# Retention into Fourier mixing with an MLP: the third batch goes to Strassen groups and a written order

## The chip, the cores and the metric

The kernel runs on one core of a Trainium2 chip. Its engines work in parallel: TensorE (PE in the profile; its weight loads are PEld), VectorE (DVE), ScalarE (ACT), GpSimd (POOL), and SyncE (SP), which here only issues DMAs. The metric is device microseconds of one execution; the time before is the median of three runs.

## The reference

Inputs are q, k, v of shape (4 batches, 8 heads, 768 rows, 64) and two MLP weights, 512 x 2048 and 2048 x 512, all float32.

```python
gamma = 1.0 - 2.0 ** (-5.0 - np.arange(H))
for t in range(S):                      # retention, per batch and head
    state = gamma * state + outer(k[t], v[t])
    y[t] = q[t] @ state / sqrt(D)
x = y with the heads side by side       # (4, 768, 512)
mixed = real(fft(fft(x, axis=1), axis=2))
u = x + mixed
un = (u - mean(u)) / sqrt(var(u) + 1e-6)          # per row
out = u + maximum(un @ w_ch1, 0) @ w_ch2
```

## The kernel before

**Attention.** The recurrence is done in six chunks of 128 rows, for two heads (a pair) at a time, four pairs per batch. `load_unit` brings q, k and v of a pair by DMA. `cast_unit` (POOL) makes f16 copies, `t_unit` transposes q and k (by PE in batches 0 and 1, by DMA from SP in batches 2 and 3). `a_unit` (L659) multiplies k and q of two chunks at a time into a PSUM tile `wkA`, and DVE multiplies that by a decay mask in float32 (`maskp`) into the f16 tile `atm`. `kv_unit` (L676) makes the states `s`: five matmuls, one ACT copy, four DVE steps. `y_unit` (L702) adds state part (ten small matmuls) and score part (twelve, reading `atm`), and ACT writes x.

**Mixing.** `fold_s`, `fold_d` and `fold_e` (DVE) fold x by its symmetries. `s1_unit` (L843) is the DFT over the sequence: six matmuls of 193 columns, four times per batch; ACT casts each result into `g`, and a reversed copy goes into `gr` (here on DVE). `s2_unit` (L993) is the DFT over the features for one block of 128 rows: four matmuls of `g` (row blocks 0 to 2) or `gr` (3 to 5), two ACT copies (`qn`), two DVE operations into `u`, two POOL additions of x. `norm_unit` (L1046) takes row statistics on DVE and writes `un` (mean minus u, f16) on ACT. `unT_unit` (L1071) transposes `un` into `unT`, by DMA from batch 2 on.

**MLP, batches 0 to 2.** `h_unit` (L1087) makes one of 16 hidden blocks for 384 rows, four matmuls of 384 columns; Relu is split between ACT (`ACT_ROWS`) and DVE. `ch_unit` (L1124) is a quarter of the second product for one block of 128 rows: four matmuls of 512 columns, and in the last quarter a DVE operation that scales by 1/std, adds u and leaves a tile `ob` for the output DMA.

**MLP, batch 3.** It goes by three groups of 256 rows. `hp_unit` (L1169) makes hidden blocks n and n + 8 for the group: eight matmuls of 256 columns and a Relu of 512 elements. The second product is a Strassen scheme: the group is seen as 2 x 2 blocks (two row blocks i and j, two halves of the hidden units), the weights likewise (two halves of the output columns). Seven products (`p_unit`, L1205) of eight 256-column matmuls each stand in for the eight of the plain form. The sums of hidden blocks are made by DVE (`hidden_sums`, L1193: s1, s2, s4 and a difference that overwrites a quarter of the hidden tile), those of weights once by DVE (`wsum_unit`, L1156: eight subtractions). After each product DVE adds its PSUM half, scaled, to u or to an output tile. Products 1, 6 and 7 add up in one PSUM half, so that product 6 waits until DVE has read product 1, and product 7 until it has read product 6.

**Order.** Every piece of work is a unit with a due time in batches: the hidden and product units of batch b (the "majors") are spread evenly over b to b + 1, and the next batch's attention and mixing lie between them at times given by tables. `emit` (L1387) sorts all units by due time and traces them in that order. A scheduler then orders each engine's instructions by priority and readiness as it foresees them; what a unit's wrapper `held` (L150) marks can't be moved ahead of the instruction traced before it on its engine. Before, `held` is around the casts and around everything of batch 3. Waits between engines are semaphores; an engine executes its queue in order. [...]

## Time and profile before

| what | us |
|---|---|
| three runs | 240.98, 240.98, 241.79 (median 240.98) |
| profiled execution | 240.73 |
| its span, first to last instruction | 238.7 |
| busy: PE, DVE, ACT, POOL | 225.4, 187.4, 125.3, 81.4 |

The span runs from the first to the last instruction of the program; the execution's own time is 2.0 us longer. In a group row of the profile stand line, engine, operation, output <- inputs and shapes, the count, the busy time in all, the mean ns of one, and the idle time of the engine just before. In the chain of work that ended last, each piece has its start, its length and its name; rows are merged when neighbours are of one kind.

### The profile page before, as it was taken

To read this page: it belongs to the slowest core of one execution; us is meant where nothing else is said; L and a number is where in the kernel's file an instruction comes from. 1 tells how busy PE (TensorE), PEld (TensorE's weight loads), DVE (VectorE), ACT (ScalarE), POOL (GpSimd) and SP (SyncE) were. 2 spreads that over 40 slices of the span, in tenths; PEclk is the share of its full clock that TensorE was granted. 3 is DMA by queue.
4 is the path that set the end of the run, shared out by engine and by line. 5 is a ranking of instruction groups with operands and counts; after the bars stand their busy time and mean duration, and the time that the engine had idled before them with its cause. 6 is when DMAs were issued, how large, how long until landed. Compare 5 with 4: busy or idle time off the path is not lost.

```text
span 238.7 us, 5575 instructions
## 1 busy us (share of the span) xinstructions
PE 225.4 (94%) x2135; PEld 155.3 (65%) x2135; DVE 187.4 (79%) x460; ACT 125.3 (52%) x273; POOL 81.4 (34%) x148
## 2 busy tenths in 40 slices
PE   0788999999999999999999999999999999999993
PEld 0356779756775646765567446655666468888893
DVE  8789887958898889986886829977895885867473
ACT  5989759674865444840247415822257326072430
POOL 8378802665300097850000826940002410220000
PEclk9999999999999999999999999999999999999999
DMA  7999999999999489979999577696100261031202
GB/s 179 233 270 239 237 206 207 210 251 248 241 235 208 72 191 221 203 138 132 249 279 218 116 161 203 130 138 156 53 3 0 45 154 25 3 110 23 91 0 91
DMA packets 100954, 36.80 MB, mean 154 GB/s; under 512 B 91456, under 2 KB 97984, under 8 KB 100928
## 3 DMA queue, kind: packets, MB, share of 16 engines
q1 hardware_dynamic: 96704, 32.25, 64.2%
q0 software_dynamic: 4224, 4.19, 10.6%
q8 instruction: 17, 0.28, 0.5%
q14 instruction: 9, 0.07, 0.1%
HBM read 27.26 MB, written 6.29 MB: 141 GB/s over the span
## 4 chain that ended last, share of the span: by engine, by line
PE 82%; DVE 6%; DMA 5%; ACT 2%; issue 1%; POOL 1%; SPq 0%; DVEq 0%; ACTq 0%
PE psc L1131 23%; PE psh L1092 21%; PE psh L1179 9%; PE ps L1231 5%; PE psh L1109 3%; PE wkA L667 3%; DMA qTz<-q16z 3%; PE ps L850 3%; DMA k<-in_k_dram 2%; PE wkY L721 2%; PE pq L1012 2%; PE ps L830 1%; DVE atm L539 1%; PE wkY L717 1%; PE wkK L686 1%
## 5 line engine op out<-in xcount | busy, mean ns | idle before, releaser
L1131 PE MATMUL psc<-w,ht 128*128 128x512 f16 x288 | 67.7, 379 | 0.0
L1092 PE MATMUL psh<-unT,w 128*128 128x384 f16 x320 | 59.5, 326 | 0.0
L1040 POOL TENSOR_TENSOR u<-u,x 128x256 f32<-128x256 f32 x21 | 13.3, 635 | 117.1 <-DVE u L1019 104.8
L1131 PEld LDWEIGHTS <-ht 128*128 128x128 f16 x288 | 27.3, 98 | 26.5
L1092 PEld LDWEIGHTS <-w 128*128 128x128 f16 x320 | 29.9, 98 | 15.9 <-DMA unT<-un 0.4
L1096 ACT ACTIVATE ht<-psh 128x384 f16<-128x384 f32 x46 | 22.3, 489 | 23.7 <-PE psh L1092 23.2
L670 DVE TENSOR_TENSOR atm<-wkA,maskp 128x512 f16<-128x512 f32 x36 | 23.6, 680 | 1.7 <-PE wkA L667 1.7
L1184 ACT ACTIVATE ht<-psh 128x512 f16<-128x512 f32 (+1 forms) x24 | 13.7, 571 | 15.6 <-PE psh L1179 11.0
L1179 PE MATMUL psh<-unT,w 128*128 128x256 f16 x192 | 21.6, 273 | 0.0
L1098 DVE TENSOR_SCALAR ht<-psh 128x384 f16<-128x384 f32 x34 | 18.7, 549 | 2.7 <-PE psh L1092 2.5
L1056 ACT ACTIVATE un<-u,stats 128x512 f16<-128x512 f32 x21 | 14.8, 717 | 10.7 <-DVE stats L1052 7.6
L1179 PEld LDWEIGHTS <-w 128*128 128x128 f16 x192 | 18.7, 98 | 2.1
L1135 DVE SCALAR_TENSOR_TENSOR ob<-psc,stats,u 128x512 f32<-128x512 f32 x18 | 13.4, 743 | 8.5 <-PE psc L1131 8.3
L696 DVE SCALAR_TENSOR_TENSOR s<-s,gk,wkK 128x128 f16<-128x128 f16 x48 | 16.1, 336 | 2.4 <-ACT s L692 1.6
L729 ACT ACTIVATE x<-wkY,gexp 128x384 f16<-128x384 f32 x24 | 12.9, 580 | 9.0 <-PE wkY L721 8.9
L1051 DVE BATCH_NORM_STATS2 bst<-u 128x6 f32<-128x512 f32 x21 | 14.4, 686 | 4.0 <-POOL u L1042 3.8
L1231 PEld LDWEIGHTS <-ht 128*128 128x128 f16 x152 | 14.1, 98 | 2.3 <-issue 0.6
L441 POOL TENSOR_SCALAR kd<-k,gexp 128x384 f16<-128x384 f32 x24 | 13.8, 585 | 3.3 <-DMA k<-in_k_dram 3.3
L667 PE MATMUL wkA<-qTz,kT 128*128 128x256 f16 x72 | 13.2, 273 | 0.3 <-DMA qTz<-q16z 0.3
L1042 POOL TENSOR_TENSOR u<-u,x 128x256 f32<-128x256 f32 x21 | 13.3, 635 | 0.0
L1014 ACT COPY qn<-pq 128x128 f32<-128x128 f32 x18 | 4.9, 274 | 15.0 <-PE pq L1012 15.0
L1203 DVE TENSOR_TENSOR ht<-ht 128x512 f16<-128x512 f16 (+2 forms) x21 | 8.1, 385 | 5.9 <-ACT ht L1184 5.6
(194 smaller groups left out, 400.9 us busy)
## 6 DMA issues: line engine op xcount, KB each, us to landing
q<-in_q_dram SPq DMA_DIRECT2D x16, 384.0 KB, 6.0
k<-in_k_dram SPq DMA_DIRECT2D x16, 384.0 KB, 5.6
v<-in_v_dram SPq DMA_DIRECT2D x16, 384.0 KB, 5.7
out_dram<-ob SPq DMA_DIRECT2D x23, 256.0 KB, 2.4
w<-in_moe_w_ch_dram POOLq DMA_DIRECT2D x8, 512.0 KB, 10.9
unT<-un SPq DMA_TRANSPOSE x15, 2.5
kT<-kd SPq DMA_TRANSPOSE x10, 3.0
qTz<-q16z SPq DMA_TRANSPOSE x8, 3.8
```

Source lines behind the costliest of these rows:

```text
L441: kc = nc.gpsimd.tensor_scalar(out=kd[:, :, h2, :], in0=k32[:, h2], scalar1=gkd[:, h0 + h2:h0 + h2 + 1], scalar2=1.0, op0=ALU.mult, op1=AL ...
L667: mm = nc.tensor.matmul(wk[:, c2], st["kT"][:, c, :], st["qT"][:, :, c, :], start=True, stop=True)
L670: nc.vector.tensor_tensor(out=st["atm"][:, 2 * part:2 * part + 2], in0=wk, in1=maskp[:, PAIR_ORDER[i]].unsqueeze(1).to_broadcast([P, 2, 2, ...
L696: nc.vector.scalar_tensor_tensor(out=s16[:, c], in0=s16[:, c - 1], scalar=gk2[:, hp:hp + 1], in1=wk[:, c - c0], op0=ALU.mult, op1=ALU.add)
L1051: nc.vector.bn_stats(bst, u[:, kb, :])
L1056: nc.scalar.activation(un, u[:, kb, :], AF.Identity, bias=stats[:, kb, 0:1], scale=-1.0)
L1092: nc.tensor.matmul(psh, w116[:, cb, fb * P:(fb + 1) * P], unT[:, cb, rt * 384:(rt + 1) * 384], start=(cb == 0), stop=(cb == 3))
L1096: nc.scalar.activation(ht16[:, fb, :], psh, AF.Relu, bias=0.0, scale=-1.0)
L1098: nc.vector.tensor_scalar(out=ht16[:, fb, :], in0=psh, scalar1=-1.0, scalar2=0.0, op0=ALU.mult, op1=ALU.max)
L1131: nc.tensor.matmul(psc, ht16[:, fb, rb3 * P:(rb3 + 1) * P], w216[:, fb, :], start=(fb == 0), stop=(fb == NFB - 1))
L1179: nc.tensor.matmul(psh[:, t], w116[:, cb, fb * P:(fb + 1) * P], unT[:, cb, g * 256:(g + 1) * 256], start=(cb == 0), stop=(cb == 3))
L1231: nc.tensor.matmul(dst, lhsT, rhs[:, c0:c1], start=bool(new and n == 0), stop=(n == 7), skip_group_check=True)
```

## The change

Batch 2 (`SEVEN = 2`, and all later ones) is now done by row groups too.

- Groups 0 and 1 of batch 2 take the seven products, group 2 takes the plain form by `cg_unit` (32 matmuls of 512 columns). Batch 2 then has 49 majors: per group 8 `hp`, one `rstd`, and 7 products or 8 plain quarters. Weight sums are due at 1.555 to 1.80 instead of 2.89 to 2.98, and go to `wide` (four of the former eleven input buffers) and to the unused tables `cd16`, `sd16`; seven input buffers remain for batch 3.
- In the groups all Relus are ACT's, hidden sums come after block 5 (blocks 0 to 5, 768 elements) and 7, and the products' order is 1, 2, 4, 6, 5, 7, 3 instead of 1, 4, 5, 6, 2, 7, 3. In batch 1 ACT also takes every Relu whose block is no multiple of 4 (27 of 32 instead of 18).
- Everything due from 2.0 on is `held` on PE, ACT, POOL and DVE.
- Batch 3's scores are read from PSUM by ACT, six reads of 256 elements a pair with the scale, and DVE masks all 1536 at once in f16. The copies into `gr` of that batch are ACT's.
- Row blocks 3, 4, 5 of batch 2 are mixed at 1.83 to 2.04 (before: within batch 2, 2.048 to 2.341); blocks 0 and 1 of batch 3 at 2.84 to 2.95 (before 2.728 to 2.815), block 2 at 3.005 to 3.15.
- Times of batch 3's attention are given one by one. With hp(b, g, n) falling due at b + k/49, the written order in batch 2 is, in group 1: a(3,2,0) 2.347, hp 0, a(3,2,1), hp 1, a(3,2,2), hp 2, kv(3,3), hp 3, a(3,3,0), hp 4, y(3,2), a(3,3,1), hp 5 2.449, a(3,3,2) 2.460, hp 6, hp 7, rstd, y(3,3) 2.530, product 1 2.531; in group 2: hp 5 2.776, s1(0,0) 2.780, hp 6, s1(1,0), s1(0,1), hp 7 2.816, s1(1,1) 2.820, rstd, s2(block 0) 2.840, plain quarter 0, s2(block 1) 2.860, quarters 1 and 2, statistics of block 0, quarter 3, statistics of block 1 2.930, its transpose 2.950, quarters 4 to 7, s2(block 2) 3.005, hp 0 of batch 3 3.021.
- There are two output tiles instead of three.

The diff, cut to its core:

```diff
-ON_ACT = {'q': (0, 1, 0), 'kv': (1, 1, 1), 'g': (0, 1, 1), 'gr': (0, 0, 0)}
+ON_ACT = {'q': (0, 1, 0), 'kv': (1, 1, 1), 'g': (0, 1, 1), 'gr': (0, 0, 1)}
+END7 = 0.75
+C7 = (-0.035, 0.025, 0.12, 0.22)
+T7 = (-0.02, 0.04, 0.185, 0.315)
+KV7 = (0.03, 0.11, 0.31, 0.39)
+A7 = ((0.04, 0.10), (0.12, 0.17), (0.33, 0.38), (0.41, 0.46))
+Y7 = (0.18, 0.305, 0.44, 0.53)
+F7 = (0.57, 0.60, 0.65, 0.67, 0.68, 0.70, 0.72)
+DA7 = (0.02, 0.07)
-LD0, LD1 = (0.223, 0.312), (-0.370, 0.140)
+LD0, LD1, LD2 = (0.223, 0.312), (-0.2425, -0.115, 0.0125, 0.14), (-0.2425, -0.115, 0.0, 0.06)
-WS = (-0.12, -0.02)
-LAST_MIX = {3: (0.0, 0.07, 0.09, 0.20), 4: (0.25, 0.34, 0.36, 0.45), 5: (0.37, 0.445, 0.51, 0.56)}
-SUMS = ((3, 7), (2, 5, 7))
+WS = (-0.48, -0.20)
+MIX = {2: {3: (-0.17, -0.11, -0.10, -0.05), 4: (-0.13, -0.06, -0.05, 0.00),
+           5: (-0.08, -0.01, 0.00, 0.04)},
+       3: {0: (-0.16, -0.09, -0.08, -0.07), 1: (-0.14, -0.07, -0.06, -0.05),
+           2: (0.005, 0.075, 0.105, 0.15), 3: (0.03, 0.115, 0.17, 0.20),
+           4: (0.25, 0.34, 0.36, 0.45), 5: (0.37, 0.445, 0.51, 0.56)}}
+SEVEN = 2
+PLAIN = ((2, 2),)
...
-    inp = pool("inp", 11)
+    inp = pool("inp", 7)
-    obp = pool("obp", 3)
+    obp = pool("obp", 2)
+    mask16 = gk5[:, 1].rearrange("p e c -> p (e c)").bitcast(f16)[:, 0:P]
...
-    def held(unit):
+    def held(unit, engines=("",)):
...
+                if not any(g in str(ins[n].engine) for g in engines):
+                    continue
...
+    wide = const.tile([P, 4, 2, NCH, D], f32, tag="wide")
+    def in_tile(name, b):
+        n = loads[0] % 11
+        loads[0] += 1
+        if b < B - 1 and n >= 7:
+            return wide[:, n - 7]
+        return inp.tile([P, 2, NCH, D], f32, tag="in32", name=f"{name}32")
...
             a_of[b, i] = mm
+            if b >= SEVEN:
+                for h2 in range(2):
+                    nc.scalar.activation(st["atm"][:, 2 * part:2 * part + 2, h2, :], wk[:, :, h2],
+                                         AF.Copy, bias=0.0,
+                                         scale=float(gam[2 * PAIR_ORDER[i] + h2] ** (-P)))
+                if part == 2:
+                    atm = st["atm"].rearrange("p c h t -> p (c h) t")
+                    nc.vector.tensor_tensor(
+                        out=atm, in0=atm, in1=mask16.unsqueeze(1).to_broadcast([P, 2 * NCH, P]),
+                        op=ALU.mult)
+                return
...
-            if fb in ACT_ROWS[rt]:
+            if fb in ACT_ROWS[rt] or b + 1 == SEVEN and fb % 4:
...
+    def cg_unit(b, g, t, part):
...
+            for fb in range(4 * part, 4 * part + 4):
+                nc.tensor.matmul(psc_of[0], hg[:, fb % 8, fb // 8, t * P:(t + 1) * P],
+                                 w216[:, fb, :], start=(fb == 0), stop=(fb == NFB - 1))
...
+            for t0, t1 in ((0, 1), (1, 2)) if n == 7 else ((0, 2),):
+                nc.scalar.activation(hg[:, n, t0:t1], psh[:, t0:t1], AF.Relu, bias=0.0,
+                                     scale=-1.0)
+            if (b, g) in PLAIN:
+                return
+            if n == 5:
+                hidden_sums(0, 6, (1, 2, 4, 3))
+            elif n == 7:
+                hidden_sums(6, 8, (1, 2))
...
         for e in ev:
-            e[3]()
+            (e[3] if e[0] < SEVEN else held(e[3], ("PE", "Act", "Pool", "DVE")))()
...
-        if b == B - 1:
+        if b >= SEVEN:
             for g in range(3):
-                majors += [held(hp_unit(b, g, n)) for n in range(8)]
-                majors.append(held(rstd_unit(b, g, 2)))
-                majors += [held(p_unit(b, g, k)) for k in (1, 4, 5, 6, 2, 7, 3)]
+                majors += [hp_unit(b, g, n) for n in range(8)]
+                majors.append(rstd_unit(b, g, 2))
+                if (b, g) in PLAIN:
+                    majors += [cg_unit(b, g, t, part) for t in range(2) for part in range(4)]
+                else:
+                    majors += [p_unit(b, g, k) for k in (1, 2, 4, 6, 5, 7, 3)]
...
+                for make, times in ((cast_unit, C7), (t_unit, T7), (kv_unit, KV7), (y_unit, Y7)):
+                    streams += [([make(b + 1, i)], b + t, b + t) for i, t in enumerate(times)]
```

More of the change, by code (lines that the diff above doesn't have):

```diff
@@ L1251, in run @@
                 add(right, ps, ri, right)
-            elif k == 5 and tail:
-                flat_dc = seven["dc"].rearrange("p t m -> p (t m)")
-                add(u[:, j, 0:384], flat_dc[:, 0:384], rj, u[:, j, 0:384])
-                add(u[:, j, 384:DM], seven["e"], rj, u[:, j, 384:DM])
             elif k == 5:
-                add(pair(u[:, j]), seven["dc"], rj, pair(u[:, j]))
+                for dst, c0, c1 in outs:
+                    uj = u[:, j, 256 + c0:256 + c1]
+                    add(uj, dst, rj, uj)
             elif k == 7:
@@ L1456 @@
             streams.append((sums, end + da[0], end + da[1]))
-            streams += mix_units(b + 1, [0, 1, 2], *(end + t for t in da[2:]))
+            if b + 1 < B - 1:
+                streams += mix_units(b + 1, [0, 1, 2], *(end + t for t in da[2:]))
     emit(streams)
```

134 lines of the change are left out of this document (76 added, 58 removed).

## The prediction

> **What bounds the kernel now.** I read the page first (busy shares, the chain's shares by engine), then busy time by stage, then the chain in order of time.
>
> ```profile
> PE 225.4 (94%) x2135; PEld 155.3 (65%) x2135; DVE 187.4 (79%) x460; ACT 125.3 (52%) x273; POOL 81.4 (34%) x148
> ...
> PE 82%; DVE 6%; DMA 5%; ACT 2%; issue 1%; POOL 1%; SPq 0%; DVEq 0%; ACTq 0%
> ```
>
> PE is busy 94% of the span and holds 82% of the chain. The stages, cut where PE turns from batch 0's first hidden units to batches 1, 2 and 3 (columns: busy us of PE, PEld, DVE, ACT, POOL, then granted clock and DMA):
>
> ```profile
> 90.40:142.40 52.00, 51.72 (x411) 31.27 (x409) 39.90 (x96) 22.74 (x55) 18.83 (x32) 1.00 0.97 189
> 142.40:194.40 52.00, 52.00 (x420) 31.99 (x420) 44.41 (x102) 22.41 (x53) 15.95 (x27) 1.00 0.46 99
> 194.40:235.00 40.60, 40.07 (x384) 35.66 (x382) 26.97 (x68) 17.03 (x36) 3.69 (x6) 1.00 0.15 49
> ```
>
> Batch 2, the stage that the change rewrites, has no idle PE at all (52.00 of 52.00). So the change can win there only matmul work, and every wait that it adds to PE's queue is added to the end. The matmul rates, from unbroken runs in the chain:
>
> ```profile
> 132.08 10.36 PE psc L1131 x48
> ...
> 163.74 0.28 PE wkK L686 x5
> ...
> 164.88 0.29 PE wkY L717 x10
> 165.17 0.35 PE wkY L721 x12
> ...
> 171.64 5.94 PE psh L1092 x36
> 177.58 0.51 PE ps L850 x6
> 178.30 1.56 PE ps L850 x18
> ...
> 183.57 0.23 PE pq L1012 x4
> ...
> 209.41 6.11 PE psh L1179 x56
> 215.53 6.23 PE ps L1231 x56
> ```
>
> A 512-column matmul takes 10.36/48 = 0.216 us, a 384-column one 5.94/36 = 0.165, a 256-column one 6.11/56 = 0.109; the seven products of one row group take 6.23. PE's waits in the second half of the span are two (columns: total us, times, longest):
>
> ```profile
> PE ps L1231 <- DVE u L1235: 0.4, 1, 0.4
> PE wkA L667 <- DMA qTz<-q16z: 0.3, 1, 0.3
> ```
>
> The first is batch 3's, behind a Strassen add; the second is batch 1's, behind a DMA transpose.
>
> **The change part by part.** *Matmul work.* Batch 2's second product now takes 96 x 0.216 = 20.7 us; afterwards two groups of seven products (2 x 6.2 = 12.4) and one plain group (32 x 0.216 = 6.9) take 19.3. The hidden layer keeps its columns: 128 x 0.165 = 21.1 becomes 192 x 0.109 = 20.9, no difference that I count. **Saved: 1.4 us.** Row blocks that move between batches change no matmul.
>
> [...]
>
> *Waits.* Before, units before batch 3 could be reordered by the scheduler; now each engine executes everything due from 2.0 on in written order. I lay the written order beside these durations:
>
> ```profile
> L670 DVE TENSOR_TENSOR atm<-wkA,maskp 128x512 f16<-128x512 f32 x36 | 23.6, 680 | 1.7 <-PE wkA L667 1.7
> ...
> L1056 ACT ACTIVATE un<-u,stats 128x512 f16<-128x512 f32 x21 | 14.8, 717 | 10.7 <-DVE stats L1052 7.6 <-issue 2.2 <-POOL u L1042 0.6
> L1051 DVE BATCH_NORM_STATS2 bst<-u 128x6 f32<-128x512 f32 x21 | 14.4, 686 | 4.0 <-POOL u L1042 3.8
> ...
> L1135 DVE SCALAR_TENSOR_TENSOR ob<-psc,stats,u 128x512 f32<-128x512 f32 x18 | 13.4, 743 | 8.5 <-PE psc L1131 8.3
> ...
> L1042 POOL TENSOR_TENSOR u<-u,x 128x256 f32<-128x256 f32 x21 | 13.3, 635 | 0.0
> ...
> L729 ACT ACTIVATE x<-wkY,gexp 128x384 f16<-128x384 f32 x24 | 12.9, 580 | 9.0 <-PE wkY L721 8.9
> L1184 ACT ACTIVATE ht<-psh 128x512 f16<-128x512 f32 x21 | 12.5, 597 | 14.8 <-PE psh L1179 10.2 <-issue 4.6
> ...
> L1019 DVE SCALAR_TENSOR_TENSOR u<-pq,g,qn 128x256 f32<-128x256 f32 x18 | 8.5, 475 | 4.3 <-PE psh L1092 2.5 <-ACT qn L1015 1.6
> ...
> L773 DVE TENSOR_TENSOR eo<-xab 128x768 f16<-128x768 f16 x12 | 6.1, 552 | 0.1
> ...
> L1015 ACT COPY qn<-pq 128x127 f32<-128x127 f32 x18 | 5.2, 287 | 0.0
> ...
> L1052 DVE BATCH_NORM_AGGREGATE stats<-bst 128x2 f32<-128x6 f32 x21 | 3.5, 173 | 0.1
> ...
> L861 DVE COPY g16r<-g 128x384 f16<-128x384 f16 x12 | 3.1, 261 | 3.0 <-ACT g L857 2.9
> ...
> L1165 DVE TENSOR_TENSOR wsum<-w,wsum 128x1024 f16<-128x1024 f16 x4 | 2.8, 688 | 0.1
> ...
> L1235 DVE SCALAR_TENSOR_TENSOR ob<-ps,stats,u 128x256 f32<-128x256 f32 x5 | 2.4, 482 | 0.9 <-PE ps L1231 0.7
> ...
> L358 ACT COPY csn<-csp 128x384 f16<-128x384 f16 x1 | 0.6, 616 | 0.0
> ```
>
> Instructions of one engine overlap a little. ACT's timeline shows by how much:
>
> ```profile
> 178.13 2.37 ACT L857 CAST g<-ps 128x386 f16<-128x386 f32 x4
> ...
> 201.42 0.38 ACT L1184 ACTIVATE ht<-psh 128x256 f16<-128x256 f32 x1 [0.28 <-PE psh L1179]
> 201.70 0.29 ACT L1066 ACTIVATE stats<-stats,epsT 128x2 f32<-128x2 f32 x1
> ```
>
> So 386-column casts follow each other after 2.37/4 = 0.6 us at most (0.55 with the overlap), a 256-column read of PSUM frees ACT after 0.28 (201.42 to 201.70), and a 512-column Relu, 597 ns long, after 0.56 to 0.6.
>
> (a) *Scores.* Per pair, three DVE products (0.68) become six ACT reads of 256 columns (0.28 each: 1.7 us) and one f16 mask of 1536 elements. No row shows that size; 768 elements take 0.55 and 1024 0.69, so the slope is 0.14 us per 256 and I take 0.95; bounds 0.69 (the 1024 row) and 2.04 (the rate of the f32 row, if the repeated mask loses the f16 rate). DVE gains 4 x (2.04 - 0.95) = 4.4 us in batch 2, ACT takes 6.8 more. DVE had 44.4 of 52 us, ACT 22.4, so there is room on average; what matters is order.
>
> (b) *The last y of batch 3's attention.* In group 1 PE's written order is a(2,0), h0, a(2,1), h1, a(2,2), h2, kv, h3, a(3,0), h4, y2, a(3,1), h5, a(3,2), h6, h7, y3, product 1, where h is eight matmuls (0.87), a two (0.22), kv 0.28, y 0.64. Counted from the first a, h5 ends at 7.26 and y3's score half comes up at 9.5. ACT has, to its fifth Relu, six Relus at 0.56 to 0.6, ten score reads at 0.28 to 0.3, one copy and two x writes at 0.5; it ends Relu 5 at 8.1 (never late) to 8.5 (waits counted). DVE then does Strassen sums of blocks 0 to 5, written behind h5: four of 768 elements, 2.1 us, and only then pair 3's mask, 0.95, written behind a(3,2). The mask ends at 11.2 to 11.6, y3 was due at 9.5: **1.7 to 2.1 us, I take 1.7**; 1.4 if the mask costs 0.69, 3.0 if it costs 2.04. y3 stands in front of product 1, so all PE work waits; no cover.
>
> (c) *Sequence DFT into feature DFT.* In group 2: h5, s1, h6, s1, s1, h7, s1, then s2 with nothing between. s2's fourth matmul reads the last s1's copy. From h5's start, PE has 4.9 us of work to the end of the last s1 (4 x 0.51 + 3 x 0.87, and 0.2 for the small sums between the rows at 177.58 and 178.30), 5.0 with the s2 matmuls that needn't wait. ACT's queue behind h6, which ends at 2.5, is Relu 6 (0.6), g, gr, g, gr (1.1 + 2 x gr), Relu 7 (0.6), g (0.6). The gr copies are new on ACT (261 ns on DVE; an f16 copy of that size took 616 on ACT): I take 0.45, bounds 0.26 and 0.62. The last g ends at 2.5 + 3.8 = 6.3, and with 0.2 for the way from PE to ACT and back at 6.5 (6.1 to 6.8): **1.5 us, 1.1 to 1.8.** In the old order PE had eight hidden matmuls between, and gr was DVE's.
>
> (d) *First hidden unit of batch 3.* Rows 0 to 255 come from s2 of blocks 0 and 1, written only at 2.84 and 2.86. From the end of block 1's s2: two ACT copies 0.6, two DVE adds of the L1019 kind 0.9, two POOL adds 1.3, on DVE the out add of row block 4 that is written ahead (0.7) and the statistics (0.9), on ACT the normalised rows (0.7), and the transpose, issue to landing:
>
> ```profile
> out_dram<-ob SPq DMA_DIRECT2D x23, 256.0 KB, 2.4
> ...
> unT<-un SPq DMA_TRANSPOSE x15, 2.5
> ```
>
> That is 0.6 + 0.9 + 1.3 + 0.7 + 0.9 + 0.7 + 2.5 = 7.6 us. PE has seven plain quarters of 4 x 0.216 and one s2 of 0.23, 6.3. **1.3 us** (0.6 without the out add, 1.9 with ACT's backlog from (c)).
>
> (e) *Product 6 behind product 1's add.* In group 0, DVE does the sums (2.1), the last sums (0.6), the mask of pair 1 (0.95) and then product 1's add, while products 2 and 4 give 1.75 us of cover: 0.4 us (0 to 0.6). In batch 3 the order 1, 2, 4, 6, 5, 7 replaces 1, 4, 5, 6, 2, 7: the wait of 0.4 behind L1235 loses 0.2 (0 to 0.4), as fewer adds now stand ahead of product 6's on DVE.
>
> (f) *At nothing.* Batch 1's 9 Relus go to ACT, which has 52.0 - 22.7 = 29 us free there. Batch 2's blocks 3 to 5 (5.4 us of DVE) and the weight sums (8 x 0.69 = 5.5) move into batch 1's second half, which 4 Relus leave. DVE's 39.9 of 52 hides it; if it doesn't, block 1's transpose for batch 2 is late, 0 to 1.5 us. Batch 3's twelve loads now share seven buffers, so the last five wait for the casts of pairs 0 and 1; the loads began long before they are needed:
>
> ```profile
> 108.45 0.57 SPq L199 DMA_DIRECT2D q<-in_q_dram x1
> ```
>
> That is 34 us ahead of batch 2, and hides them; a late one delays a DMA transpose, which cost 0.3 in the one case above. The transposes of pairs 2 and 3 have 7 and 6 us of PE work between their issue and their readers. Two output tiles do where three were: one is written every 16 x 0.216 = 3.5 us at most, and its DMA lands after 2.4.
>
> **Sum:** -1.4 + 1.7 + 1.5 + 1.3 + 0.4 - 0.2 = +3.3 us on the profiled execution's 240.73 (span 238.7 and 2.0 around it): **244.0**. The median of the runs shown, 240.98, lies 0.25 above that execution. With all low ends (1.4, 1.1, 0.6, 0, -0.4) +1.3, 242.0; with all high ends (3.0, 1.8, 1.9, 0.6, 0, and 1.5 from (f)) +7.4, 248.1.
>
> **The rivals.** *Covered (faster).* PE's matmul work decides, because ACT and DVE run ahead of it: y3's mask lands before h7 ends and the s1 copies are out before h7's Relu. It decides if (b), (c) and (d) together stay under 1.4 us, which needs the mask ahead of the sums or ACT at half the time per read. For it: PE idles nowhere in batches 2 and 3 now. Against it: that was with free order. -1.4 - 0.2: **239.1**. *A wash.* (b) alone or (c) with (d) alone stands: 240.73 - 1.6 + 2.0 = **241.1**. *Crowded.* DVE saturates in batch 1 (1.5, from (f)) and the mask runs at the f32 rate (1.3 more in (b)): **246.8**. *Not what it says:* with 98 ns a weight load (PEld 35.7 of 40.6 in batch 3) 256-column matmuls could be load-bound; then nothing is saved and the forecast is 245.4; the 0.109 above already holds this, so it has no chance of its own.
>
> *Clock.* Where PE has no work, the granted clock falls, as the last slice shows:
>
> ```profile
> 235.00:240.00 5.00, 0.00 (x0) 0.00 (x0) 0.31 (x2) 0.00 (x0) 0.00 (x0) 0.89 0.24 80
> ```
>
> Two waits close together, (c) and (d), could do the same; 0.89 over the 5 us that follow costs 0.6, so **244.6**. [...]
>
> **How the numbers follow.** Forecast 0.58, covered 0.14, wash 0.18, crowded 0.07, clock 0.03. A measurement of this kernel can tell 0.5% (1.2 us) from no change: below 239.8 is faster, above 242.2 slower. Of the forecast, 0.02 falls below 242.2. So faster 0.14, same 0.20, slower 0.66. The range leaves out some of the covered case and the last of the crowded: 239.8 to 246.6.
>
> **What would show it.** Right: in batch 2 PE idles behind DVE atm for over 1.4 us once, behind ACT g for over 1 us before a pq matmul, and behind the unT transpose before the first hidden unit of batch 3; psc matmuls fall to 224. Wrong: PE busy over 51 us of that stage, or new waits elsewhere (transposes of q and k, input loads, output tiles).

## The result, and the profile after

The changed kernel takes 247.93 us (median of four runs, 247.32 to 250.01) against 240.98: a ratio of 1.0298, interval 1.0232 to 1.0364. That is slower, as forecast, but by 7 us instead of 3.3, and 1.3 above the end of the range. The profiled execution took 247.62 us, its span is 245.7 instead of 238.7.

First the busy times on the page of the changed kernel, and three of its groups (columns as before: count, busy us, mean ns, idle time ahead):

```profile
PE 226.8 (92%) x2247; PEld 166.9 (68%) x2247; DVE 178.7 (73%) x437; ACT 150.6 (61%) x351; POOL 87.3 (36%) x148
...
L700 ACT ACTIVATE atm<-wkA 128x256 f16<-128x256 f32 x48 | 16.2, 397 | 5.1 <-PE wkA L695 5.1
...
L705 DVE TENSOR_TENSOR atm<-atm,gk 128x1536 f16<-128x1536 f16 x8 | 8.2, 1022 | 9.6 <-ACT atm L700 9.6
...
L466 POOL TENSOR_SCALAR q16z<-q 128x384 f16<-128x384 f32 x14 | 10.0, 731 | 10.8 <-DMA q<-in_q_dram 10.5
```

DVE lost 8.7 us of work and ACT took 25.3 more. The counts are the surprise: 48 score reads and 8 masks are those of two batches, not one. The switch in the code is `b >= SEVEN`, so it covers batch 2 as well, and the `gr` copies of batch 2 follow the same index. **The section on the change and the prediction say "batch 3" there; that was a misreading of mine.** The attention of batch 2 runs during batch 1, so batch 1 got 24 reads, 4 masks and 4 copies that no step of the sum has.

Busy time by stage of the changed kernel, cut at the same places of the work as before (batches 0, 1, 2, 3; the first cut starts at 38 us):

```profile
38.00:90.90 52.90, 52.31 (x534) 35.38 (x532) 43.59 (x111) 32.76 (x65) 21.59 (x33) 1.00 1.02 205
90.90:146.20 55.30, 53.49 (x425) 32.24 (x423) 42.18 (x92) 36.09 (x98) 34.81 (x50) 1.00 1.05 200
146.20:201.20 55.00, 50.02 (x513) 41.71 (x511) 35.41 (x86) 33.32 (x84) 4.67 (x8) 1.00 0.28 71
201.20:242.00 40.80, 40.35 (x388) 36.09 (x388) 25.19 (x64) 18.37 (x40) 4.61 (x8) 1.00 0.16 49
```

Batch 2 takes 55.0 us instead of 52.0 though PE has less to do in it, and batch 1 takes 55.3 instead of 52.0, where ACT went from 22.7 to 36.1 busy us and POOL from 18.8 to 34.8. The granted clock is 1.00 everywhere. PE's waits (total us, times, longest), without those of the first 40 us and without one of 0.2 that was there before:

```profile
PE wkY L760 <- DVE atm L705: 2.8, 3, 1.8
PE psh L1236 <- DMA unT<-un: 1.5, 1, 1.5
PE pq L1051 <- ACT g L896: 1.2, 1, 1.2
PE ps L1289 <- DVE u L1293: 0.9, 3, 0.4
PE psh L1131 <- ACT ht L1135: 0.8, 2, 0.4
...
PE psh L1131 <- DVE ht L1137: 0.3, 1, 0.3
```

The three largest stand on PE's timeline of batch 2 (start, length; in brackets the idle time just before and its releaser):

```profile
172.29 0.46 PE L756 MATMUL wkY<-s,qTz 128*128 128x64 f16 x10
174.54 0.52 PE L760 MATMUL wkY<-v,atm 128*128 128x64 f16 x12 [1.80 <-DVE atm L705]
...
190.59 0.33 PE L1051 MATMUL pq<-gk,g 128*128 128x129 f16 x3
192.17 0.23 PE L1051 MATMUL pq<-gk,g 128*128 128x128 f16 x1 [1.24 <-ACT g L896]
...
199.37 0.40 PE L1051 MATMUL pq<-gk,g 128*128 128x129 f16 x4
201.25 0.93 PE L1236 MATMUL psh<-unT,w 128*128 128x256 f16 x7 [1.48 <-DMA unT<-un]
```

They are the three waits that the forecast named, at their places. Below I use *pauses*: the time from the start of one matmul to the start of the next, less what a matmul of that width takes in an unbroken run. They come out some 0.17 us above the idle times in brackets, since those are counted from the modelled end of the last matmul.

| | forecast | measured |
|---|---|---|
| matmul work without pauses (217.59 to 216.16) | -1.4 | -1.43 |
| (b) last y of batch 3, at 172.5 us | +1.7 | +1.96 |
| (c) second DFT step, at 190.7 | +1.5 | +1.41 |
| (d) first hidden unit of batch 3, at 199.5 | +1.3 | +1.64 |
| (e) product 6 in batch 2, at 158.0; a product in group 1, at 180.0 | +0.4; 0 | +0.51; +0.32 |
| (e) product 6 in batch 3 (0.59 to 0.53) | -0.2 | -0.06 |
| (f) batch 1 (pauses 0.93 to 3.35) | 0 | +2.4 |
| batch 0, the pauses after 40 us | none | +0.5 |

These add up to +7.3; small pauses that are fewer than before bring it to the span's +7.0. Batch 1's are 0.58 at 99.0 us (behind ACT's Relu), 0.71 at 101.4 and 0.64 at 121.5 (a y of batch 2 behind the mask), 0.46 at 125.0 (behind DVE's Relu) and some 0.45 between 128 and 130.

### The profile page after: what moved, and what is told of

Same layout as the page of the kernel before. It is cut to its first block, busy times and chain, and to the rows that moved or that the text cites. A ratio compares the mean times of both kernels' runs of the same rounds, so it can differ in the third digit from the quotient of the medians.

```text
span 245.7 us, 5860 instructions
## 1 busy us (share of the span) xinstructions
PE 226.8 (92%) x2247; PEld 166.9 (68%) x2247; DVE 178.7 (73%) x437; ACT 150.6 (61%) x351; POOL 87.3 (36%) x148
## 5 line engine op out<-in xcount | busy, mean ns | idle before, releaser
L1236 PE MATMUL psh<-unT,w 128*128 128x256 f16 x384 | 45.7, 273 | 1.5 <-DMA unT<-un 1.5
L1170 PE MATMUL psc<-w,ht 128*128 128x512 f16 x192 | 45.8, 379 | 0.0
L1240 ACT ACTIVATE ht<-psh 128x512 f16<-128x512 f32 (+1 forms) x54 | 29.2, 554 | 25.3 <-issue 16.4
L1236 PEld LDWEIGHTS <-w 128*128 128x128 f16 x384 | 37.2, 98 | 6.0 <-issue 1.6
L1131 PE MATMUL psh<-unT,w 128*128 128x384 f16 x192 | 36.2, 326 | 1.1 <-ACT ht L1135 0.8
L1131 PEld LDWEIGHTS <-w 128*128 128x128 f16 x192 | 17.9, 98 | 10.4 <-issue 1.6
L1259 DVE TENSOR_TENSOR ht<-ht 128x768 f16<-128x768 f16 (+1 forms) x30 | 12.3, 421 | 10.8 <-ACT ht L1240 10.5
L700 ACT ACTIVATE atm<-wkA 128x256 f16<-128x256 f32 x48 | 16.2, 397 | 5.1 <-PE wkA L695 5.1
L1289 PE MATMUL ps<-wide,ht 128*128 128x256 f16 x120 | 15.1, 272 | 0.7 <-DVE u L1293 0.7
L705 DVE TENSOR_TENSOR atm<-atm,gk 128x1536 f16<-128x1536 f16 x8 | 8.2, 1022 | 9.6 <-ACT atm L700 9.6
L466 POOL TENSOR_SCALAR q16z<-q 128x384 f16<-128x384 f32 x14 | 10.0, 731 | 10.8 <-DMA q<-in_q_dram 10.5
L695 PE MATMUL wkA<-qTz,kT 128*128 128x256 f16 x72 | 13.4, 273 | 0.0
```

The source lines that it names most:

```text
L695: mm = nc.tensor.matmul(wk[:, c2], st["kT"][:, c, :], st["qT"][:, :, c, :], start=True, stop=True)
L700: nc.scalar.activation(st["atm"][:, 2 * part:2 * part + 2, h2, :], wk[:, :, h2], AF.Copy, bias=0.0, scale=float(gam[2 * PAIR_ORDER[i] + h2 ...
L1131: nc.tensor.matmul(psh, w116[:, cb, fb * P:(fb + 1) * P], unT[:, cb, rt * 384:(rt + 1) * 384], start=(cb == 0), stop=(cb == 3))
L1170: nc.tensor.matmul(psc, ht16[:, fb, rb3 * P:(rb3 + 1) * P], w216[:, fb, :], start=(fb == 0), stop=(fb == NFB - 1))
L1236: nc.tensor.matmul(psh[:, t], w116[:, cb, fb * P:(fb + 1) * P], unT[:, cb, g * 256:(g + 1) * 256], start=(cb == 0), stop=(cb == 3))
L1240: nc.scalar.activation(hg[:, n, t0:t1], psh[:, t0:t1], AF.Relu, bias=0.0, scale=-1.0)
```

## The experiments

The theory after the result: batch 2's part is the three waits as forecast, and batch 1's part is a crowd on ACT, DVE and POOL from work that was moved there. The rivals: that one piece alone makes batch 1's loss (the reads on ACT, the blocks, the weight sums, the casts on POOL); and that the waits of batch 2 are not three addends but members of one chain (scores, y, fold, DFT, transpose, first hidden unit), so that what one gives the next takes.

### What makes batch 1's loss

**Scores and copies of batch 2 back on DVE.**

```diff
-            if b >= SEVEN:
+            if b > SEVEN:
...
-                (nc.scalar.copy if ON_ACT["gr"][min(b, 2)] else nc.vector.tensor_copy)(
+                (nc.scalar.copy if b > 2 and ON_ACT["gr"][min(b, 2)] else nc.vector.tensor_copy)(
```

> The changed kernel, but batch 2's scores (made during batch 1) are again masked by DVE from PSUM in one step and that batch's reversed copies into gr are DVE's; batch 3 keeps ACT. Theory A: of the 7.0 us lost, about 2.4 are waits of PE in batch 1 that come from work put on ACT there (24 x 2 score reads of 0.39 us for batches 2 and 3 together, Relus and gr copies). Then this run wins 1 to 2 us back, 246.0 to 247.0, and PE's waits behind atm in batch 1 (1.0 us of the 2.8) go. Rival B: the batch 1 waits come from DVE's new work there (weight sums and blocks 3 to 5), then taking 12 products of 0.68 back to DVE makes it worse, 248.5 to 250.

247.39 us, ratio 1.0273 (1.0242 to 1.0303). The pauses at 99 and 101 us are gone, with 0.24 to 0.26 left. Those from 119 to 132 us shrink as well, from 1.6 to 0.5 in all, although POOL's casts, the blocks, the weight sums and the new Relu split stay in batch 1. In the stage PE has 0.28 us without work left, instead of 1.81:

```profile
90.90:146.20 55.30, 55.02 (x447) 33.90 (x444) 46.76 (x105) 28.41 (x70) 34.52 (x51) 1.00 0.99 198
```

But the third hidden unit of batch 2 now waits for DVE, and product 6 waits 1.14 instead of 0.51. PE's waits of this run:

```profile
PE ps L1289 <- DVE u L1293: 1.5, 3, 1.0
...
PE psh L1236 <- DVE ob L1174: 0.4, 1, 0.4
```

So batch 2's reads and copies on ACT carry most of batch 1's loss: without them some 1.9 of the 2.4 us are gone. Of these only some 0.5 us comes back in the time. The rest, 0.60 and 0.63, went into DVE's queue at the start of batch 2.

**The Relu split back as well.** To the last run is added:

```diff
-            if fb in ACT_ROWS[rt] or b + 1 == SEVEN and fb % 4:
+            if fb in ACT_ROWS[rt]:
```

> As the first run, and the Relus of batch 1 divided between ACT and DVE as in the kernel before (18 of 32 on ACT). Theory A: batch 1's waits fall to about 1 us as before, 245.5. Rival B (DVE is what is short in batch 1's second half): DVE now has all its old work of batch 1 plus the weight sums and three blocks, and the time is 248 to 250.

247.59 us, ratio 1.0281 (1.0253 to 1.0309): no gain. Its stage from 90.9 to 146.2 us, and the wait that is new:

```profile
90.90:146.20 55.30, 53.55 (x427) 32.40 (x425) 50.39 (x114) 24.58 (x61) 33.19 (x50) 1.00 1.06 201
```

```profile
PE psh L1131 <- DVE ht L1137: 1.2, 2, 0.8
```

DVE is now busy 50.4 of 55.3 us, PE waits for DVE's Relus (0.56 and 0.98), and batch 1's pauses are nearly back at what they were. So once the scores are DVE's, the Relus have to stay with ACT: DVE cannot take both beside the blocks and the weight sums.

**Batch 3's casts held behind POOL's additions.** In the changed kernel each cast of batch 3 is held behind what was traced before it, but the first, due at 1.965, isn't held, and the rest follow it: POOL begins the four pairs between 113 and 140 us, beside batch 1.

```diff
-                    streams += [([make(b + 1, i)], b + t, b + t) for i, t in enumerate(times)]
+                    streams += [([held(make(b + 1, i)) if make is cast_unit else make(b + 1, i)],
+                                 b + t, b + t) for i, t in enumerate(times)]
```

> The changed kernel, but POOL's casts of batch 3's first two pairs may not be moved ahead of the additions for batch 2's row blocks 3 to 5, so that they no longer run beside DVE's weight sums and folds. Theory D: POOL's casts slow DVE's f16 operations with two SBUF inputs (one 1024-element weight sum took 1.09 us instead of 0.68, a 768-element fold 0.93 instead of 0.55, a mask 1.28 instead of 0.96, each beside a cast); then those durations return to 0.68, 0.55 and 0.96, and of batch 1's waits 0.3 to 0.8 us go: about 247.3. Theory A alone: the durations have another cause and stay, and the time stays at 247.9, or grows by up to 1 us as transposes come later.

256.8 us, ratio 1.0665 (1.0639 to 1.069). What this costs is late transposes:

```profile
PE wkA L695 <- DMA kT<-kd: 5.7, 2, 3.7
...
PE wkK L725 <- POOL v L474: 0.9, 1, 0.9
```

The waits are not all. In this run TensorE's granted clock is halved for 3.4 us from 149.9 us on, during the second of two pauses close together (1.1 at 147 us, 2.1 at 150), and again from 160.2 us on, behind a pause of 3.9. That costs 1.4 and 1.7 us. The second time, as a row of the stages:

```profile
160.20:162.00 1.80, 1.77 (x9) 1.27 (x10) 0.35 (x1) 0.66 (x2) 0.00 (x0) 0.50 1.08 247
```

In batch 1, where nothing but POOL's casts is gone, the pauses at 121 to 131 us fall from 0.64, 0.46 and some 0.45 to 0.32, 0.23 and 0.29. So about 0.7 of the 2.4 us went with the casts; by how much DVE and the casts slow each other is in the last section. The size is rough: in the runs further down that edit batch 2 alone, with the casts in place, the pauses from 119 to 132 us add up to between 1.2 and 1.9, against 1.6 in the changed kernel and 0.8 here. And the casts cost this only together with the f16 mask behind ACT's reads: in the first run they stand at nearly the same times, the masks read PSUM again, and these pauses are 0.5. Starting the casts early is right all the same: it is worth 9 us here, 3.1 of them by the clock.

**Blocks 3 to 5 of batch 2 back in batch 2.**

```diff
-MIX = {2: {3: (-0.17, -0.11, -0.10, -0.05), 4: (-0.13, -0.06, -0.05, 0.00),
-           5: (-0.08, -0.01, 0.00, 0.04)},
+MIX = {2: {3: (0.015, 0.075, 0.09, 0.15), 4: (0.195, 0.255, 0.27, 0.32),
+           5: (0.235, 0.295, 0.31, 0.36)},
```

> The changed kernel, but row blocks 3 to 5 of batch 2 are mixed in batch 2 again (due 2.015 to 2.36). Theory G (DVE and ACT together are crowded in batch 1, about 3.4 us of PE waits where 0.9 were): the waits between 121 and 131 us were before these blocks' time and stay, so the gain is small, 247.3 to 247.9, and batch 2 may lose as much. Rival H: these blocks are the crowd; 246.0.

249.59 us, ratio 1.0366 (1.0344 to 1.0388). Batch 1's pauses at 121 to 131 us fall to 0.32, 0.23 and 0.29, the same as with the casts held back. The edit moves more than it says: POOL's additions for the blocks now stand ahead of casts 1 to 3, which the trace shows at 147 us and later instead of 121 to 140. So it doesn't tell the blocks from the casts in batch 1; the run before, with the blocks in place and the same pauses, speaks for the casts. In batch 2 it costs more than it gives:

```profile
PE wkA L695 <- DMA kT<-kd: 1.4, 1, 1.4
```

**And the weight sums later.** To the last run is added `WS = (-0.20, 0.05)` instead of `(-0.48, -0.20)`.

> As the run before it, and the weight sums are due at 1.83 to 2.05 instead of 1.555 to 1.80. Theory G: with 5.5 us of DVE gone from 119 to 132 us, the waits at 121 to 131 (1.7 us) fall to below 0.7; 246.4 to 247.0, if DVE in batch 2's first group has room. Rival: POOL's casts, which run then, and not DVE's amount of work, make these waits; they stay.

250.22 us, ratio 1.0393 (1.0371 to 1.0416). Batch 1's pauses stay as in the run before (0.32, 0.22, 0.38): with the casts and blocks out of batch 1, the weight sums have no part in them.

**All of it back at once:** the edits of the first two runs, the blocks' and the sums'.

> All extra work of batch 1 is taken back at once: batch 2's scores and copies on VectorE as before, the Relu split as before, blocks 3 to 5 of batch 2 back in batch 2, the weight sums in batch 2. What stays in batch 1 beside its own work are the casts of batch 3 on GpSimd. Theory A (batch 1's 2.4 us come from the sum of the added pieces, none of them alone): TensorE's waits between 91 and 146 us fall to 1.3 or less together, while batch 2, which gets the pieces back, loses 2 to 4 us more; time 248.5 to 250.5. Rival (the casts on GpSimd beside VectorE are enough by themselves): the waits in that stage stay at 2 or more, time 250 to 252.

248.84 us, ratio 1.0339 (1.0318 to 1.0359). The pauses between 91 and 146 us are 0.33, 0.22 and 0.53, near the 0.93 of before: what was moved into batch 1 is the cause. But the first run, which took back scores and copies alone, left no more (0.24, 0.26, 0.22 and 0.20), so this run does not show that all pieces are needed. Against what I wrote ahead of it, the casts did not stay on POOL in batch 1 (again the additions hold them back), and batch 2 pays for that: a pause of 1.1 behind POOL's cast of v at 150 us, 1.0 behind a transpose at 152, and 1.2 behind a Strassen add at 162.

### Are batch 2's three waits one chain?

**Mask ahead of the sums.** The last score part is due at 2.447 instead of 2.46, so that its mask comes before Strassen's hidden sums on DVE:

```diff
-A7 = ((0.04, 0.10), (0.12, 0.17), (0.33, 0.38), (0.41, 0.46))
+A7 = ((0.04, 0.10), (0.12, 0.17), (0.33, 0.38), (0.41, 0.447))
```

> The changed kernel, but the last score step of batch 3's last pair is written one place earlier, ahead of hidden block 5 of group 1, so that its mask stands ahead of the Strassen sums on DVE. Theory E (one chain): the waits before the last y (1.96 us), the first feature DFT (1.41) and batch 3's first hidden unit (1.64) are one chain from that mask to batch 3, longer than PE's work beside it. The mask comes 2 us earlier and the chain with it: the first wait goes and the other two don't grow; 246.0. Rival F (separate waits against fixed times on other engines): the wait goes but comes back before batch 3's first hidden unit, as in the run with free order, where 1.2 us saved there came back as 1.5; then 247.5 to 248.

246.55 us, ratio 1.0241 (1.0219 to 1.0263). The pause at the last y is gone (1.96 to 0), so step (b) had its cause right. (c) and (d) are unchanged at 1.40 and 1.65, and the products pay more than half of it back: in group 1 they now wait 0.23, 0.78 and 0.46 instead of 0.32.

```profile
PE ps L1289 <- DVE u L1293: 1.6, 4, 0.6
```

**Copies of the first DFT step on DVE:** `'gr': (0, 0, 0)`.

> The changed kernel, but all reversed copies into gr are DVE's again. Theory E: three of them, 0.51 us each, stand on ACT ahead of the last cast before the feature DFT; without them that wait of 1.41 us falls to about 0.4 (two of the three copies were in its way), the wait before batch 3's first hidden unit stays at 1.6 or falls by the last copy's 0.4: 246.3 to 247.0. Rival F: the second wait grows by what the first loses, 247.9.

246.87 us, ratio 1.0259 (1.0211 to 1.0307). The pause of (c) falls from 1.41 to 0.77, that of (d) from 1.64 to 1.46. ACT's timeline of the changed kernel, just ahead of the second DFT step, shows what is taken out:

```profile
190.56 0.51 ACT L900 COPY g16r<-g 128x384 f16<-128x384 f16 x1
190.98 0.65 ACT L1240 ACTIVATE ht<-psh 128x256 f16<-128x256 f32 x2
191.52 0.59 ACT L896 CAST g<-ps 128x386 f16<-128x386 f32 x1
```

A copy takes 0.51 us and the next cast follows the copy and the Relus, as the queue of step (c) had it.

**Batch 2 in free order.**

```diff
-            (e[3] if e[0] < SEVEN else held(e[3], ("PE", "Act", "Pool", "DVE")))()
+            (e[3] if e[0] < SEVEN + 1 else held(e[3], ("PE", "Act", "Pool", "DVE")))()
```

> The changed kernel, but only what falls due from 3.0 on is held in written order; batch 2 may be reordered by the scheduler. Theory A: the wait of 2.0 us in front of the last y of batch 3's attention comes from the written order alone, since products 1 and 2 may now pass it: it goes; the waits before the first feature DFT (1.4) and before batch 3's first hidden unit (1.6) are a chain longer than the work beside it and shrink together by at most 1. So 245.0 to 246.0. Rival C: the scheduler's own order makes as many waits elsewhere in batch 2, and the time stays within 1 us of the changed kernel.

248.25 us, ratio 1.0294 (1.0255 to 1.0332): no gain in the median. The scheduler takes two products ahead of the y, whose pause falls to 0.76, and that of (c) to 0.75. But the first hidden unit of batch 3 then waits 3.14 instead of 1.64:

```profile
PE psh L1236 <- DMA unT<-un: 3.0, 1, 3.0
```

The three sum to 4.65 instead of 5.01. Here they behave as a chain: filling PE's early gaps with other work leaves the chain as late as it was.

The time is not the pauses alone, though. Over the whole span they are 1.0 less than in the changed kernel, and still the span is 0.7 longer. Behind the wait of 3.0 us the granted clock is halved for 3.4 us (matmuls of 256 columns start 213 ns apart instead of 109), and that costs 1.7:

```profile
202.00:204.00 2.00, 2.00 (x12) 1.39 (x10) 1.55 (x4) 0.80 (x4) 1.03 (x2) 0.50 0.00 0
```

The one execution of the four whose mean clock was 1.000 took 246.68 us; the other three, at 0.991 to 0.993, took 248.06 to 248.45. So the written order does cost something, about 1 us by the pauses and by that execution, and the clock hides it in the others.

**No Strassen in batch 2.**

```diff
-PLAIN = ((2, 2),)
+PLAIN = ((2, 0), (2, 1), (2, 2))
```

> All three row groups of batch 2 use the plain second product (no sums of the hidden units, no weight products in seven parts there); everything else as changed. TensorE's own work rises by about 1.4 us. Theory A (the sums on VectorE are what holds up the mask of batch 3's last scores, and product 6's wait is Strassen's own): the wait of 1.96 us ahead of the last y falls to under 0.8 and the product waits of 0.51 and 0.32 go, so 246.0 to 247.3. Rival (one latency chain from batch 3's loads to its first hidden unit: what is gained at the y comes back at the second DFT step or at the transposed units): those two waits grow by what the y loses, the time is 247.5 to 248.8.

246.76 us, ratio 1.0256 (1.0204 to 1.0308). The matmul work rises by 1.59 (to 217.75). The y's pause and the products' pauses of batch 2 are gone, (c) falls to 0.47, and (d) rises to 2.02, by 0.4. Something new comes up at the start of batch 2, a pause of 2.08 behind the last output addition of batch 1:

```profile
PE psh L1236 <- DVE ob L1174: 1.9, 1, 1.9
PE psh L1236 <- DMA unT<-un: 1.9, 1, 1.9
```

DVE's timeline says what that addition itself waits for:

```profile
148.86 0.75 DVE L1174 SCALAR_TENSOR_TENSOR ob<-psc,stats,u 128x512 f32<-128x512 f32 x1 [2.49 <-DMA out_dram<-ob]
```

It is an output tile: both of the two are still being written out, and DVE stands idle for 2.5 us. So this pause is a price of two output tiles instead of three, which (f) put at nothing.

**The chain earlier.** Everything late in batch 3's attention, to the transposes of blocks 0 and 1, is due 0.02 to 0.05 of a batch earlier, and the copies are on DVE as above:

```diff
...
+T7 = (-0.02, 0.04, 0.185, 0.29)
+KV7 = (0.03, 0.11, 0.29, 0.36)
+A7 = ((0.04, 0.10), (0.12, 0.17), (0.30, 0.345), (0.37, 0.41))
+Y7 = (0.18, 0.285, 0.405, 0.485)
+F7 = (0.525, 0.555, 0.605, 0.625, 0.635, 0.655, 0.675)
+END7 = 0.705
...
+       3: {0: (-0.205, -0.135, -0.125, -0.115), 1: (-0.185, -0.115, -0.105, -0.095),
```

> Everything of batch 3's attention that comes late in batch 2 (last two pairs' transposes, scores, y, the folds, both DFT steps, norm and transposes of blocks 0 and 1) is put 0.025 to 0.05 of a batch earlier in the written order (1.3 to 2.5 us), and the copies of the first DFT step go back to VectorE in batch 3. Theory A (latency chain that starts too late): the three waits at the y, the second DFT step and the first hidden unit, together 5.0 us, fall to 2 or less, and the time is 244.3 to 245.5. Rival (VectorE's queue is what is full at that place, so an earlier place only moves the wait to the products): the products' waits grow from 0.8 to 2 or more, and the time is 246.3 to 248.

243.52 us, ratio 1.0108 (1.0087 to 1.0128): 4.4 us better than the change as it was. All three pauses are gone; the timeline of PE shows the second DFT steps and the first hidden unit of batch 3 without a wait:

```profile
189.31 0.40 PE L1051 MATMUL pq<-gk,g 128*128 128x129 f16 x4
...
197.32 0.40 PE L1051 MATMUL pq<-gk,g 128*128 128x129 f16 x4
197.55 1.04 PE L1236 MATMUL psh<-unT,w 128*128 128x256 f16 x8
```

The products of batch 2 pay 2.0 us of pauses instead of 0.8 (0.42, 0.35, 0.78, 0.46), because scores, mask and folds now stand ahead of their sums and adds on DVE. So both readings hold in part: one chain that started too late, and behind it a DVE queue.

### Both, and what is left

**No Strassen in batch 2 and the chain earlier.**

> Both of the two: no Strassen in batch 2 and the late part of batch 3's attention earlier, copies of the first DFT step on VectorE. Theory A of both: the three waits fall to 1.5 or less, product waits gone, matmul work 1.4 more than as changed: 243.8 to 245.3. If batch 1's waits of 2.4 us and batch 0's of 0.5 are all that is left of the loss, 243.5. Rival (chain): 246 to 248.

243.14 us, ratio 1.0098 (1.0075 to 1.0121). The products' pauses are gone and the matmul work is 1.59 more: the time is that of the last run within the intervals. Strassen in batch 2 is worth nothing in this pair of runs: its products save 1.59 us of matmul work, and they bring pauses of 2.0 us with them.

**The same with batch 2's scores on DVE.**

> The run with both (no Strassen in batch 2, late part of batch 3's attention earlier, copies of the first DFT step on VectorE) and batch 2's scores on VectorE as before. The first of these runs left TensorE's waits of 0.56 at 62 us (batch 0), 0.59 and 0.70 at 99 and 101 us, 0.32 to 0.69 at 121 to 128 us. Theory (what is left of the loss is batch 1's load, and with VectorE free of the hidden sums in batch 2 there is nothing behind it to which the waits can move): the waits at 99 and 101 us go and do not come back, time 241.3 to 242.4. Rival (as with the scores alone, the work moved to VectorE comes back as a wait at the start of batch 2): 242.8 to 243.8.

242.52 us, ratio 1.0052 (1.0025 to 1.0079), the best of all versions and still not under the kernel before. It came out between what the two readings gave. The pauses at 99 and 101 us are gone, with 0.24 and 0.32 left; and 0.82 comes up at 146 us:

```profile
PE psh L1236 <- DVE ob L1174: 0.7, 1, 0.7
```

Here the account closes. The span is 240.6, 1.9 above before; matmul work is 0.16 more, the first 40 us 0.15, and the pauses are 0.56 at 62, 0.24 at 103 and 0.82 at 146: 1.9.

**The same with the Relu split back and the weight sums in batch 2** (`WS = (0.30, 0.60)`).

> The kernel of the run before in this call, and also the Relu split of batch 1 as before and the weight sums moved from batch 1 to the second half of batch 2 (only batch 3 needs them here). Of the change's extra work batch 1 then keeps blocks 3 to 5 of batch 2 and the casts of batch 3 on GpSimd. Theory (the account is complete: matmul work as before, no extra wait but batch 0's 0.5 and a little in batch 1): 240.7 to 242.0. Rival (VectorE in batch 1 is too full with its own Relus, scores and the blocks of batch 2, as when scores and Relus were taken back without the rest): waits at VectorE's Relu of 0.5 to 1.5 at 123 to 127 us stay, time 242.2 to 243.5.

244.23 us, ratio 1.0117 (1.0074 to 1.0161), worse. Pauses of 1.17 and 0.98 stand at 146 to 149 us and one of 0.96 at 116:

```profile
PE psh L1236 <- DVE ob L1174: 1.8, 2, 1.0
```

DVE is late into batch 2, and the pause at 116 is a late transpose in batch 1. Moving work back to DVE does not pay even where Strassen has left batch 2; two edits are in this run, so it doesn't say which of them does it.

**Chain earlier, Strassen kept, batch 2's scores on DVE.**

> The run with the late part of batch 3's attention earlier, Strassen in two row groups of batch 2 kept, and batch 2's scores on VectorE as before. Theory (batch 1's two waits behind ScalarE, 1.3 us, are an addend of their own): 241.9 to 242.9. Rival (VectorE's queue at the start of batch 2 takes them over, since the sums and adds of Strassen stand there): waits of the products 2.5 or more instead of 2.0, a wait at about 146 us, and 243.2 to 244.2, no gain against the run without this edit.

243.59 us, ratio 1.0091 (1.006 to 1.0122): no gain on the run without this edit (243.52). Batch 1's two pauses shrink to 0.24 and 0.20, product 6 of group 0 waits 1.00 instead of 0.42, and in the profiled execution the first 40 us were 0.5 longer, with a wait for a weight load:

```profile
PE ps L1289 <- DVE u L1293: 2.3, 5, 0.8
PE psh L1148 <- DMA w<-in_moe_w_ch_dram: 0.8, 1, 0.8
```

## Why the prediction was wrong, by its own steps

- **Matmul work: right.** -1.43 measured, -1.4 forecast; the spacings of 216 and 109 ns from the rows of before carry over.
- **(a) The price of the scores: right, and applied to the wrong batches.** A mask that nothing disturbs takes 0.95 us, as estimated; a read frees ACT after 0.26 to 0.28; a `gr` copy takes 0.51 instead of 0.45.
- **(b): right in cause, 0.26 too small.** DVE's timeline of the changed kernel has the queue as written, four sums and then the mask:

```profile
171.40 1.15 DVE L1259 TENSOR_TENSOR ht<-ht 128x768 f16<-128x768 f16 x2 [2.33 <-ACT ht L1240]
172.58 0.56 DVE L1259 TENSOR_TENSOR s4t<-ht 128x768 f16<-128x768 f16 x1
173.06 0.55 DVE L1259 TENSOR_TENSOR ht<-ht 128x768 f16<-128x768 f16 x1
173.53 0.95 DVE L705 TENSOR_TENSOR atm<-atm,gk 128x1536 f16<-128x1536 f16 x1
```

  Taking the mask ahead of the sums removed the whole wait, and moved 1.2 us of it to the products.
- **(c), (d): right within 0.1 and 0.35.** What the sum did not say is how they hang together: started earlier, all three go at once; the gaps filled, as in free order, they come back at the last one. The 0.2 in (c) for the way from PE to ACT and back was an estimate of mine that no row ahead of it shows; the changed kernel's trace has about 0.1: 0.04 from the modelled end of a score matmul (163.45) to ACT's read (163.49), and 0.06 from the end of ACT's last `g` (192.11) to the matmul that waits for it (192.17).
- **(e): right** (0.51 for 0.4), but a second product wait of 0.32 was not seen, and batch 3's gain was 0.06 instead of 0.2.
- **(f) "At nothing": this step failed, and with it the number.** It put at nothing what moves into batch 1 and the loss of the third output tile. Batch 1 cost +2.4 and the output tile +0.5, together 2.9 of the 4.0 us by which the loss exceeds the forecast; the rest is 0.3 each in (b) and (d) and 0.4 in (e).
  - *Work that no step had.* It priced nine Relus, the blocks and the weight sums, and missed batch 2's scores, masks and copies. ACT has 13.4 us more to do in the stage, and 11.5 of them are these and the Relus (24.6 with all of them back on DVE). With scores and copies back, batch 1's pauses fell by 1.9 of the 2.4 us.
  - *Shares instead of queues.* It said that DVE's 39.9 of 52 us and ACT's 29 free us hide the rest, which is the argument that the prediction refused elsewhere. ACT is busy 36.1 of 55.3 us in the stage and DVE 42.2, so neither is full; PE waits because a mask or a Relu comes late in its engine's queue, not because the engine has no time. POOL's casts, moved in from batch 2, slow DVE at the same time (a mask beside two casts took 1.28 us instead of 0.96; some 0.7 us of pauses beside the reads).
  - *What it priced and what did not come.* The end of its range, 1.5, was from a transpose that would be late; no such wait came up. The weight sums cost nothing that can be seen.
- **Batch 0's 0.5 belongs to (f) too: "two output tiles do where three were".** It is one pause of 0.57 at 62 us, where a hidden unit waits for ACT's Relu, and it stood in every version, as did the two tiles. The traces show where it comes from. PE and ACT run alike in both kernels up to there, but DVE's third output addition of the batch stands at 59.34 us before and at 64.44 after (first line before, second after):

```profile
59.34 0.74 DVE L1135 SCALAR_TENSOR_TENSOR ob<-psc,stats,u 128x512 f32<-128x512 f32 x1
```

```profile
64.44 0.74 DVE L1174 SCALAR_TENSOR_TENSOR ob<-psc,stats,u 128x512 f32<-128x512 f32 x1
```

  With two tiles it has to wait for the first one's output DMA, which SyncE issues only at 56.5 us and which lands 5.9 us later, at 62.35. Until the addition is done, its PSUM tile is one of the three that the kernel gives the MLP (`ps_pm`), so the next hidden unit waits for ACT instead of taking it (again before, then after):

```profile
62.25 0.81 PE L1092 MATMUL psh<-unT,w 128*128 128x384 f16 x4
```

```profile
62.86 0.81 PE L1131 MATMUL psh<-unT,w 128*128 128x384 f16 x4 [0.40 <-ACT ht L1135]
```

  The step reckoned with 2.4 us to landing, which is the median before (2.7 for the same transfers in the changed kernel); the longest is 5.9. No run was made with three tiles and the rest of the change.
- **The signs and the range.** The signs of being right all came up: waits of 1.80, 1.24 and 1.48 us at the three places, and 224 `psc` matmuls. All three lie in batch 2, so they could not tell that batch 1 was missing. Of the signs of being wrong, one came up, the output tiles. The sum of all high ends (+7.4) covers the measured +7.0, but not by its own terms: (b) to (e) stayed below their high ends, and (f) went over its 1.5.
- **Rivals.** The clock rival is out for the changed kernel (1.00 in each stage). Where longer waits did lower the clock, in two of the experiments, it was halved for 3.4 us and cost 1.4 to 1.7, not the 0.6 of its sum. "Crowded" had the right stage and about the right time (246.8), but DVE did not saturate there, and nearly half of its loss stood on the mask at the f32 rate, which did not happen (0.95 us, not 2.04). "Covered" is what the earlier chain nearly shows: its condition was the mask ahead of the sums and the copies done early, and with both the three waits go. It stayed at 243.5 instead of 239.1, because of batch 1 and of the products' waits.

## What to carry to other kernels

Work that is moved "under cover" needs the same treatment as work on the critical path: lay it into the queue of each engine of the stage that receives it, in order, and check with the counts in the code for which iterations a switch holds. The same holds for buffers: count when the transfer that frees one really lands (5.9 us here), not the median (2.4). When several waits follow each other on one chain, try the start of the chain first: here that gave 4.4 us, single members 1.1 to 1.4, and filling the gaps with other work sent part of the wait down the chain. A scheme that saves matmuls and adds VectorE work gained nothing here: 1.59 us of matmul work saved, 2.0 of pauses behind the adds, which stand between two matmul groups.

## What the runs showed of the hardware

In batch 1 of the changed kernel DVE and POOL slow each other down, and only in some operations. DVE's timeline with POOL's casts beside it:

```profile
121.00 1.28 DVE L705 TENSOR_TENSOR atm<-atm,gk 128x1536 f16<-128x1536 f16 x1 [1.19 <-ACT atm L700]
122.20 0.98 DVE L1224 TENSOR_TENSOR cd<-w 128x1024 f16<-128x1024 f16 x1
```

```profile
120.97 1.69 POOL L466 TENSOR_SCALAR q16z<-q 128x384 f16<-128x384 f32 x2 [0.38 <-POOL v L474]
```

The run with the casts held back, the same two DVE operations with POOL idle, and two casts later on:

```profile
121.04 0.96 DVE L705 TENSOR_TENSOR atm<-atm,gk 128x1536 f16<-128x1536 f16 x1 [1.19 <-ACT atm L700]
121.92 0.69 DVE L1224 TENSOR_TENSOR cd<-w 128x1024 f16<-128x1024 f16 x1
```

```profile
144.33 0.98 POOL L466 TENSOR_SCALAR q16z<-q 128x384 f16<-128x384 f32 x2
```

The mask goes from 0.96 to 1.28 us, the sum from 0.69 to 0.98, two casts from 0.98 to 1.69. Two DVE operations that read PSUM are not slower in this kernel: the add of the second DFT step takes 477 ns on average after and 475 before, and the Relu 552 and 549; in the changed kernel the six of these adds that ran wholly beside a busy POOL after 85 us took 470 on average, and the eight beside an idle one 483. The times of the mask and the two casts lie nearer to turns than to side by side: the first cast takes 0.51 us (120.97 to 121.48), as such casts do on average before (510 ns), and the mask is late by 0.32; the second, begun at 121.44, takes 1.21 and ends when the mask has been over for 0.4. Mask and two casts, from 120.97 to 122.66, took 1.69 us; one after the other they would be 0.96 + 0.98 = 1.94, side by side 0.98. What makes them slow each other is not shown.

In two runs a long wait of PE cost more than itself. With free order and with the casts held back, the granted clock is halved for 3.4 us behind a wait of 3.0 us, behind one of 3.7, and during the second of two waits of 0.9 and 2.0 within 4.2 us; each time 1.4 to 1.7 us are lost. The mean clock of the four executions with the casts held back was 0.984 to 0.987. Single waits of 1.8 to 1.9 us in other runs left it alone: the mean clock of the profiled execution was 0.999 in the changed kernel (1.80, and 1.00 in each stage) and 1.000 without Strassen in batch 2 (1.9). No run shows how long a wait has to be for it.
